# Float64 words of the weights made float32 by a scaling and three VectorE passes in place of a magnitude and four

## The chip, the cores and the metric

The kernel runs on one core of a Trainium2 chip. The core has a matrix engine (TensorE, written PE in the profile), a vector engine (VectorE, DVE), a scalar engine (ScalarE, ACT), GpSimd (POOL) and an engine that issues the transfers (SyncE, SP). Each takes its own instructions in the order in which the program gives them and waits at semaphores for the others. The metric is the device time of one execution in microseconds (us); lower is better.

## The reference

A windowed attention with global tokens, then two feed-forward layers over the 4 x (512 + 32) = 2176 token rows that the attention gives. Cut to what matters:

```
# attention: B=4, H=8, 512 local and 32 global tokens, head size 64, window 32
s_g   = scale * q_g @ concat(k_g, k_l)^T          ; out_g = softmax(s_g) @ concat(v_g, v_l)
s_l   = concat(scale * q_l @ k_g^T, where(|i - j| <= 32, scale * q_l @ k_l^T, -1e9))
out_l = softmax(s_l) @ concat(v_g, v_l)
x = concat(out_g, out_l) -> [2176, 512]
# first feed-forward layer, d_model 512, d_ff 2048
h = max(x @ w_in, 0);  x = (h * h) @ w_out
# second one
h = x @ w2_in
g = (a0 + a1*h + a2*h^2 + a3*h^3) / (1 + |b0|*|h| + |b1|*h^2 + 1e-6)
out = g @ w2_out
```

The four weight matrices arrive as float64. The chip's engines work in float32, so the kernel makes float32 words of the two 32-bit halves of each float64 word itself.

## The kernel before, in words

The order of the work is written out by hand: the program is one list, and each engine runs its own part of the list in that order.

**Attention, p = 0 to 15, and two more steps in which it drains.** Each `p` is a pair of heads. PE makes `scores` of two halves u = 0, 1; DVE finds their `maxima` (L308); ACT takes `exps` (L316); DVE adds 1e-9 to the sums (`sums`, L320) and takes their reciprocal (`norm`, L324); POOL multiplies the probabilities by it (L327, four instructions for a half); one step later PE transposes them (`transp`, L345 and L346), ACT and DVE copy the transposes out (L350, L352), and PE multiplies them by v (`pv`). On odd `p` the scores of the global queries (`g_scores`, L413 and L414) come between. They overwrite the banks that `maxima(p, 0, 0)` and `maxima(p, 0, 1)` read.

**Feed-forward.** The tokens are five tiles (512, 512, 384, 384, 384) for each of the two layers, and a tile goes through the 16 blocks of the hidden size (`s` counts tiles times blocks). At each `s` PE makes h for block s (`mm1`, L168 to L170) and the output product of block s - 3 (`mm2`, L181, LAG = 3). Every float32 product is made of three: x and the weights are split into a high and a low part. In the first layer ACT takes `max(h, 0)` out of PSUM (L210), DVE squares it (L211), ACT squares it again rounded to the high part `gh` (L212), and DVE subtracts to get the low part `gl` (L213), which `mm2` needs for its last eight products of a step.

**Weights.** There are 64 blocks of [128, 512] weights: 16 for `w_in` and 16 for `w_out` of each layer. A block is loaded by SP as 512 float64 words in each partition (`w_load`, three buffers `raw`). ACT takes the magnitude of the upper halves, read as float32 (`w_abs`, L90). DVE then makes four passes over `cv` (`w_float`): a floor (L101), a mask and a shift by 3 bits (L103), the sign and the top exponent bit from the upper halves (L105), three more mantissa bits from the lower halves (L108). After that the block is split: ACT writes the high part (L119; DVE in the attention, L117) and POOL subtracts for the low part (`w_rest`, L125). 13 of the 64 blocks are made in the attention, one for each `p` from 3 to 15, with the four passes placed apart as `step(0)` to `step(3)`. 19 more are made during the first token tile, in turns two and one for each `s`, ahead of `ew1(s)` on DVE:

```
            mm1(s)
            if j >= LAG:
                mm2(s - LAG)
            if t < NT - 1:
                floats(1)
            (ew1 if s < S1 else ew2)(s)
            if t < NT - 1:
                splits()
                if t == 0 and todo and todo[0][0] == 0:
                    magnitudes(2 - j % 2)
```

The other 32, of the second layer, are made in the tiles after that, and stored to memory until their turn.

Of the kernel before, what the change touches and what calls it, by code (L numbers as in the profile page):

```python
# [11 lines left out]
F32 = mybir.dt.float32  # L12
# [4 lines left out]
AF = mybir.ActivationFunctionType  # L17
ALU = mybir.AluOpType
# [24 lines left out]
EPS1 = 1.0 + 1e-6  # L43
SH = 60
N_IN0, N_OUT0 = 8, 5
TINY = float(np.array(0x38000000, np.uint32).view(np.float32))


def window(w):
# [4 lines left out]
def body(ctx, tc, qT, kW, v, w1i, w1o, w2i, w2o, coef, out):  # L54
    nc = tc.nc
    pe, act, dve, pool, sync = nc.tensor, nc.scalar, nc.vector, nc.gpsimd, nc.sync
# [21 lines left out]
    raws, cvs, have = {}, {}, {}  # L78
    stash = [[dram.tile([128, 512], F32, name=f"st{k}_{j}") for j in range(KF)] for k in range(2)]

    def w_load(ph, kind, j):
        raw = raw_p.tile([128, 512], I64, tag="raw", name="raw")
        src = ((w1i, w2i), (w1o, w2o))[kind][ph]
        sync.dma_start(raw, src[j])
        words = raw.bitcast(I32).rearrange("p (n t) -> p n t", t=2)
        raws[ph, kind, j] = words[:, :, 1], words[:, :, 0]

    def w_abs(ph, kind, j):
        f = t_p.tile([128, 512], F32, tag="t", name="cv")
        act.activation(f, raws[ph, kind, j][0].bitcast(F32), AF.Abs)  # L90
        cvs[ph, kind, j] = f

    def w_float(ph, kind, j, steps=(0, 1, 2, 3)):


        f = cvs[ph, kind, j]
        u = f.bitcast(I32)
        top, low = raws[ph, kind, j]
        for k in steps:
            if k == 0:  # L100
                dve.tensor_scalar(f, f, TINY, None, op0=ALU.max)  # L101
            elif k == 1:
                dve.tensor_scalar(u, u, 0x07FFFFFF, 3, op0=ALU.bitwise_and, op1=ALU.logical_shift_left)  # L103
            elif k == 2:
                dve.scalar_tensor_tensor(u, in0=top, scalar=-0x40000000, in1=u,  # L105
                                         op0=ALU.bitwise_and, op1=ALU.bitwise_or)
            else:
                dve.scalar_tensor_tensor(u, in0=low, scalar=29, in1=u,  # L108
                                         op0=ALU.logical_shift_right, op1=ALU.bitwise_or)
                del raws[ph, kind, j]  # L110
# [152 lines left out]
    def open_ff():  # L263
        qk_s.close()
        ff_p["ab"] = ctx.enter_context(tc.tile_pool(name="ab", bufs=2, side="right"))
        ff_p["g"] = ctx.enter_context(tc.tile_pool(name="g", bufs=LAG + 1, side="right"))
# [4 lines left out]
    def load_qk(p):  # L271
        b, hp = divmod(p, 4)
        qt[p] = qk_p.tile([128, SL + SG], F32, tag="q", name="q")
        kt[p] = qk_p.tile([128, KC], F32, tag="k", name="k")
        cuts = [(0, 0), (256, 576), (SL + SG, KC)] if p == 0 else [(0, 0), (SL + SG, KC)]
        for (q0, k0), (q1, k1) in zip(cuts, cuts[1:]):
            sync.dma_start(qt[p][:, q0:q1], qT[b, hp][:, q0:q1])
            sync.dma_start(kt[p][:, k0:k1], kW[b, hp][:, k0:k1])

    def load_v(g):  # L280
        b, hf = divmod(g, 2)
        vt[g] = v_p.tile([128, VC], F32, tag="v", name="v")
        sync.dma_start(vt[g], v[b, hf])
# [3 lines left out]
    def sm_tiles(p, u):  # L287
        sm[p, u] = (sm_p.tile([128, 2 * KW, 2], F32, tag="sm", name="sm"),
                    st_p.tile([128, 4], F32, tag="nm", name="nm"),
                    st_p.tile([128, 4], F32, tag="sum", name="sum"),  # L290
                    st_p.tile([128, 4], F32, tag="rs", name="rs"))

    def scores(p, u):
        for i in range(2):
            for j in range(2):
                for a in range(2):
                    r, w = slice(64 * j, 64 * j + 64), 4 * u + 2 * i + (a if i else 1 - a)
                    c = window(w) - 32 * i
                    pe.matmul(s_ps[2 * u + j][64 * a:64 * a + 64, KW * i:KW * i + KW],  # L299
                              qt[p][r, 64 * w:64 * w + 64], kt[p][r, c:c + KW],  # L300
                              start=True, stop=True, tile_position=(64 * j, 64 * a))

    def maxima(p, u, j):
        s, nm = sm[p, u][:2]
        for i in range(2):
            b, k = 2 * u + i, 2 * j + i
            o = s[:, KW * i:KW * i + KW, j]
            dve.tensor_tensor_reduce(out=o, in0=s_ps[2 * u + j][:, KW * i:KW * i + KW], in1=mask[:, b],  # L308
                                     scale=-0.125, scalar=3.0e38, op0=ALU.add, op1=ALU.min,
                                     accum_out=nm[:, k:k + 1])  # L310
# [8 lines left out]
    def sums(p, u):  # L319
        dve.tensor_scalar(sm[p, u][3], sm[p, u][2], 1e-9, None, op0=ALU.add)  # L320
# [130 lines left out]
    with tc.manual_schedule():  # L451
# [32 lines left out]
        early = [(0, 0, j) for j in range(N_IN0)] + [(0, 1, j) for j in range(N_OUT0)]  # L484
# [3 lines left out]
        for p in range(NP + 2):  # L488
            if p == NP:
                open_ff()  # L490
            if 1 <= p and p + 3 < NP:
                load_qk(p + 3)
            if p == 1:
                load_v(1)
            if p >= 4 and p % 2 == 0 and p // 2 < NP // 2:
                load_v(p // 2)
            if 1 <= p < 1 + len(early):
                w_load(*early[p - 1])
            n = p - 3
            cv = early[n] if 0 <= n < len(early) else None  # L500
            cur, pre = p < NP, 1 <= p <= NP
            odd = p % 2 == 1 and p + 2 < NP
            g = (p + 1) // 2

            def step(*k):
                if cv:
                    w_float(*cv, k)

            if cur:
                sm_tiles(p, 0)  # L510
                scores(p, 0)
                maxima(p, 0, 0)
                exps(p, 0, 0)
            else:
                mm1(p - NP)
            if 2 <= p:
                pv_local(p - 2, 0)
            if pre:
                sums(p - 1, 1)
            if cur:  # L520
                maxima(p, 0, 1)
            if pre:
                norm(p - 1, 1)
                p_tiles(p - 1, 0)
                p_tiles(p - 1, 1)
                if p > 1:
                    g_copies(p - 1, 0)
                    g_copies(p - 1, 1)
            step(0)
            if 2 <= p:  # L530
                pv_global(p - 2, 0)
            step(1)
            if p == 1:
                for k in range(4):
                    pe.matmul(tc_ps[0], warm[:, 0:128], warm, start=True, stop=True)
            if pre:
                transp(p - 1, 0)
                transp_evac(p - 1, 0)
            step(2)
            if cur:  # L540
                exps(p, 0, 1)
            if odd or p == 0:
                g_scores(g)
            if p == 1:
                g_transp(0)
                g_copies(0, 0)
                g_copies(0, 1)
            if 2 <= p:
                pv(p - 2, 1)
            if p % 2 == 0 and 0 < p < NP:  # L550
                g_transp(g)
            if cur:
                sm_tiles(p, 1)
                scores(p, 1)
                if odd or p == 0:
                    g_scale(g)
                    g_exps(g)
                maxima(p, 1, 0)
                sums(p, 0)
                step(3)  # L560
                norm(p, 0)
                exps(p, 1, 0)
                maxima(p, 1, 1)
            if odd or p == 0:
                g_norm(g)
            if cv:
                w_split(*cv, dve)
                w_rest(*cv)
            if 2 <= p:
                pv_local(p - 2, 1)  # L570
                pv_global(p - 2, 1)
            if pre:
                transp(p - 1, 1)
                transp_evac(p - 1, 1)
            if cur:
                exps(p, 1, 1)
            if pre:
                pv(p - 1, 0)
            if 0 <= n + 1 < len(early):
                w_abs(*early[n + 1])  # L580
            if 9 < p <= 9 + KD:
                x_low(0, p - 10)
            if 9 <= p < 9 + KD:
                x_high(0, p - 9)
            if p >= NP:
                ew1(p - NP)
# [26 lines left out]
        todo = []  # L613
# [22 lines left out]
        def magnitudes(k):  # L636
            for _ in range(k):
                if todo:
                    w_abs(*todo[0])
                    made.append(todo.pop(0))  # L640

        def splits():
# [25 lines left out]
        for s in range(2, 2 * S1):  # L668
            t, j = divmod(s, KF)
# [97 lines left out]
```

## Time and profile before

| | |
|---|---|
| time, median of 3 runs | 907.04 us (907.02 to 907.33) |
| the profiled execution's own time | 906.48 us |
| its span in the trace | 904.7 us |
| PE busy | 890.2 us (98%) |
| DVE busy | 662.7 us (73%) |
| ACT busy | 547.3 us (60%) |
| POOL busy | 258.8 us (29%) |

A busy share is a mean over the whole span. PE's share is high, but its instructions are pipelined, so one that waits for its operand can still count as busy; the other engines have stretches in which they are full and others in which they have little to do. The span is 1.8 us shorter than the time of the same execution, which holds what lies around it.

### The profile page before, as it was taken

What the parts mean: (1) busy time and instruction counts of PE and PEld (TensorE: products, weight loads), DVE (VectorE), ACT (ScalarE), POOL (GpSimd) and SP (SyncE); (2) the same over time, 40 slices, a digit from 0 to 9 for tenths busy, and PEclk for the clock granted to TensorE, in tenths of its full rate; (3) what the DMA queues carried; (4) which work ended last, traced back from release to release, by engine and by line L of the source; (5) the groups of instructions that cost most, each with busy time, mean ns of one, the idle gap of its engine ahead of it and who ended that gap; (6) DMA issues with size and microseconds to landing.
All of it is one profiled execution on the core that took longest, in us unless ns stands there. A gap on an engine that the chain in (4) does not pass through costs nothing.

```text
span 904.7 us, 14722 instructions
## 1 busy us (share of the span) xinstructions
PE 890.2 (98%) x5397; PEld 783.4 (87%) x5398; DVE 662.7 (73%) x1406; ACT 547.3 (60%) x1186; POOL 258.8 (29%) x324
## 2 busy tenths in 40 slices
PE   8999999997999999999999999999999999999998
PEld 4777778886888899999999978888888999999998
DVE  4788976999776568664332479877877888887886
ACT  5878874444433334342244568767766886886885
POOL 3667881334000000000036543221222222222221
PEclk9999999999999999999999999999999999999999
DMA  9767631333154327532014410001000100000001
GB/s 350 297 220 299 218 135 61 127 117 132 49 169 139 105 75 214 166 91 84 1 59 122 125 34 1 1 0 47 1 1 0 48 1 1 35 1 21 15 1 36
DMA packets 27576, 81.43 MB, mean 90 GB/s; under 512 B 3184, under 2 KB 4976, under 8 KB 26480
## 3 DMA queue, kind: packets, MB, share of 16 engines
q1 hardware_dynamic: 27504, 80.49, 26.3%
q8 instruction: 42, 0.69, 0.3%
q14 instruction: 30, 0.25, 0.1%
HBM read 67.64 MB, written 12.85 MB: 89 GB/s over the span
## 4 chain that ended last, share of the span: by engine, by line
PE 86%; DVE 10%; ACT 1%; issue 1%; DMA 1%; POOL 1%; SPq 0%; DVEq 0%; POOLq 0%; ACTq 0%
PE tc L181 19%; PE pv L181 19%; PE s L168 12%; PE s L169 12%; PE s L170 12%; PE pv L364 3%; PE tc L345 2%; DVE cv L105 2%; PE pv L370 2%; PE s L299 2%; DVE cv L101 2%; DVE cv L108 1%; DVE gl L213 1%; PE s L413 1%; DVE cv L103 1%
## 5 line engine op out<-in xcount | busy, mean ns | idle before, releaser
L168 PE MATMUL s<-xh,wi 128*128 128x384 f32 (+1 forms) x640 | 229.7, 359 | 0.0
L170 PE MATMUL s<-xh,wi 128*128 128x384 f32 (+1 forms) x640 | 228.4, 357 | 0.0
L169 PE MATMUL s<-xl,wi 128*128 128x384 f32 (+1 forms) x640 | 228.3, 357 | 0.0
L248 POOL TENSOR_TENSOR gl<-tt,gh 128x384 fp32r<-128x384 f32 (+1 forms) x79 | 89.9, 1137 | 268.1 <-ACT gh L247 207.0
L181 PE MATMUL tc<-gh,wo 128*128 128x384 f32 (+1 forms) x640 | 153.3, 361 | 0.8 <-ACT gh L247 0.8
L181 PE MATMUL pv<-gh,wo 128*128 128x384 f32 (+1 forms) x640 | 152.5, 360 | 0.0
L210 ACT ACTIVATE a<-s 128x384 f32<-128x384 f32 (+1 forms) x80 | 42.5, 532 | 153.1 <-PE s L170 153.0
L170 PEld LDWEIGHTS s<-xh,wi 128*128 128x128 f32 x640 | 120.1, 188 | 11.4
L169 PEld LDWEIGHTS s<-xl,wi 128*128 128x128 f32 x640 | 120.2, 188 | 10.8
L168 PEld LDWEIGHTS s<-xh,wi 128*128 128x128 f32 x640 | 120.1, 188 | 10.6
L181 PEld LDWEIGHTS tc<-gh,wo 128*128 128x128 f32 x640 | 116.4, 188 | 12.6 <-ACT gh L247 1.7
L181 PEld LDWEIGHTS pv<-gh,wo 128*128 128x128 f32 x640 | 115.9, 188 | 11.8
L211 DVE TENSOR_TENSOR b<-a 128x384 f32<-128x384 f32 (+1 forms) x80 | 50.3, 629 | 103.2 <-ACT a L210 103.2
L125 POOL TENSOR_TENSOR wi<-raw,wi 128x512 fp32r<-128x512 f32 x16 | 21.4, 1337 | 267.2 <-ACT wi L119 247.2
L181 PE MATMUL tc<-gl,wo 128*128 128x384 f32 (+1 forms) x320 | 89.9, 362 | 4.6 <-DVE gl L213 4.6
L181 PE MATMUL pv<-gl,wo 128*128 128x384 f32 (+1 forms) x320 | 89.8, 361 | 0.0
L225 DVE SCALAR_TENSOR_TENSOR a<-a,nf,b 128x384 f32<-128x384 f32 (+1 forms) x80 | 53.4, 667 | 32.3 <-ACT b L223 32.2
L327 POOL TENSOR_SCALAR sm<-sm,rs 128x160 f32<-128x160 f32 x128 | 63.6, 521 | 38.1 <-DVE rs L324 13.1
L222 ACT ACTIVATE a<-s 128x384 f32<-128x384 f32 (+1 forms) x80 | 42.0, 525 | 52.8 <-PE s L170 52.8
L181 PEld LDWEIGHTS tc<-gl,wo 128*128 128x128 f32 x320 | 58.7, 188 | 11.3 <-DVE gl L213 5.5
L238 DVE SCALAR_TENSOR_TENSOR a<-a,b 128x384 f32<-128x384 f32 (+1 forms) x80 | 49.0, 612 | 22.0 <-ACT b L233 22.0
L181 PEld LDWEIGHTS pv<-gl,wo 128*128 128x128 f32 x320 | 58.9, 188 | 5.9
(115 smaller groups left out, 1449.7 us busy)
## 6 DMA issues: line engine op xcount, KB each, us to landing
v<-in_v_dram SPq DMA_DIRECT2D x8, 1408.0 KB, 7.9
k<-in_kW_dram SPq DMA_DIRECT2D x15, 592.0 KB, 5.6
raw<-in_w1i_dram SPq DMA_DIRECT2D x16, 512.0 KB, 5.1
raw<-in_w1o_dram SPq DMA_DIRECT2D x16, 512.0 KB, 3.5
raw<-in_w2i_dram SPq DMA_DIRECT2D x16, 512.0 KB, 3.9
st<-cv SPq DMA_DIRECT2D x32, 256.0 KB, 4.2
raw<-in_w2o_dram SPq DMA_DIRECT2D x16, 512.0 KB, 4.0
raw<-st SPq DMA_DIRECT2D x32, 256.0 KB, 2.6
```

The lines of the kernel that those rows point to most:

```text
L168: pe.matmul(ph, wh, hi[:, kk, :n], start=(kk == 0), stop=False)
L169: pe.matmul(ph, wh, lo[:, kk, :n], start=False, stop=False)
L170: pe.matmul(ph, wl, hi[:, kk, :n], start=False, stop=(kk == KD - 1))
L181: pe.matmul(acc_bank[d][:, :n], w[:, half, 128 * d:128 * d + 128], src[:, :n], start=start, stop=stop)
L210: act.activation(a, ph, AF.Relu)
L211: dve.tensor_tensor(b, a, a, op=ALU.mult)
L222: act.activation(a, ph, AF.Square)
L225: dve.scalar_tensor_tensor(a, in0=a, scalar=nf[:, 5:6], in1=b, op0=ALU.mult, op1=ALU.add)
L238: dve.scalar_tensor_tensor(a, in0=a, scalar=EPS1, in1=b, op0=ALU.add, op1=ALU.mult)
L248: eng.tensor_tensor(gl, t, gh.bitcast(F32), op=ALU.subtract)
L327: pool.tensor_scalar(e, e, rs[:, k:k + 1], 1.0, op0=ALU.mult, op1=ALU.mult)
L364: pe.matmul(bank[64 * j:64 * j + 64, o0:o1], v[:, VW * w + 64 * jj:VW * w + 64 * jj + 64], p1[:, j, o0 + (32 if o0 >= 128 else 0):o1 + (32 ...
```

## The change

What it does: ACT no longer takes the magnitude of the upper half but multiplies it by 2^-112, with its sign. That puts the exponent where a shift by 3 bits needs it. The floor pass goes, and the mask in front of the shift goes; the shift alone is the first pass now. The second pass takes the sign bit alone from the upper half, and the third is the last one of before. In the attention, `step(0)` to `step(2)` issue the three passes, and `step(3)`, which stood between `sums(p, 0)` and `norm(p, 0)`, is gone.

```
-    def w_abs(ph, kind, j):
+    def w_scale(ph, kind, j):
         f = t_p.tile([128, 512], F32, tag="t", name="cv")
-        act.activation(f, raws[ph, kind, j][0].bitcast(F32), AF.Abs)
+        act.activation(f, raws[ph, kind, j][0].bitcast(F32), AF.Copy, scale=2.0 ** -112)
         cvs[ph, kind, j] = f

-    def w_float(ph, kind, j, steps=(0, 1, 2, 3)):
+    def w_float(ph, kind, j, steps=(0, 1, 2)):
...
             if k == 0:
-                dve.tensor_scalar(f, f, TINY, None, op0=ALU.max)
+                dve.tensor_scalar(u, u, 3, None, op0=ALU.logical_shift_left)
             elif k == 1:
-                dve.tensor_scalar(u, u, 0x07FFFFFF, 3, op0=ALU.bitwise_and, op1=ALU.logical_shift_left)
-            elif k == 2:
-                dve.scalar_tensor_tensor(u, in0=top, scalar=-0x40000000, in1=u,
+                dve.scalar_tensor_tensor(u, in0=top, scalar=-0x80000000, in1=u,
                                          op0=ALU.bitwise_and, op1=ALU.bitwise_or)
             else:
                 dve.scalar_tensor_tensor(u, in0=low, scalar=29, in1=u,
                                          op0=ALU.logical_shift_right, op1=ALU.bitwise_or)
...
                 sums(p, 0)
-                step(3)
                 norm(p, 0)
```

The lines of the changed file stand one to three lower from here on (L105 is L103, L108 is L106, L308 is L306, L320 is L318, L324 is L322, L211 is L209). On DVE, in one step of the attention (p = 12), this stood between the reciprocal of the step before and that of this one. cv and raw are the block in conversion, p and x are the attention's copies, sm, nm, sum and rs those of the softmax:

```order
L101 TENSOR_SCALAR cv<-cv 128x512
L396 COPY x<-pv_94 128x32
L103 TENSOR_SCALAR cv<-cv 128x512
L352 COPY p_1695<-tc_93 128x128
L105 SCALAR_TENSOR_TENSOR cv<-raw,cv 128x512
...
L320 TENSOR_SCALAR rs<-sum 128x4
L108 SCALAR_TENSOR_TENSOR cv<-raw,cv 128x512
L324 RECIPROCAL rs<-rs 128x4
```

The same place on DVE in the changed kernel (left out in both are the maxima of the first bank of half 1):

```order
L101 TENSOR_SCALAR cv<-cv 128x512
L394 COPY x<-pv_94 128x32
L103 SCALAR_TENSOR_TENSOR cv<-raw,cv 128x512
L350 COPY p_1686<-tc_93 128x128
L106 SCALAR_TENSOR_TENSOR cv<-raw,cv 128x512
...
L318 TENSOR_SCALAR rs<-sum 128x4
L322 RECIPROCAL rs<-rs 128x4
```

A two-source pass now stands ahead of the copy of the transposes, where the mask and shift stood, and nothing of the conversion is left between `sums` and the reciprocal.

On DVE in the first token tile, one step with two conversions before, between the elementwise work of one block and that of the next (b, gl: the square and its low part):

```order
L211 TENSOR_TENSOR b_2409<-a_2408 128x512
L213 TENSOR_TENSOR gl_2411<-b_2409,gh_2410 128x512
L101 TENSOR_SCALAR cv_2418<-cv_2418 128x512
L103 TENSOR_SCALAR cv_2418<-cv_2418 128x512
L105 SCALAR_TENSOR_TENSOR cv_2418<-raw_2356,cv_2418 128x512
L108 SCALAR_TENSOR_TENSOR cv_2418<-raw_2356,cv_2418 128x512
L101 TENSOR_SCALAR cv_2420<-cv_2420 128x512
L103 TENSOR_SCALAR cv_2420<-cv_2420 128x512
L105 SCALAR_TENSOR_TENSOR cv_2420<-raw_2362,cv_2420 128x512
L108 SCALAR_TENSOR_TENSOR cv_2420<-raw_2362,cv_2420 128x512
L211 TENSOR_TENSOR b_2459<-a_2458 128x512
L213 TENSOR_TENSOR gl_2461<-b_2459,gh_2460 128x512
```

The same step on DVE in the changed kernel:

```order
L209 TENSOR_TENSOR b_2391<-a_2390 128x512
L211 TENSOR_TENSOR gl_2393<-b_2391,gh_2392 128x512
L101 TENSOR_SCALAR cv_2400<-cv_2400 128x512
L103 SCALAR_TENSOR_TENSOR cv_2400<-raw_2340,cv_2400 128x512
L106 SCALAR_TENSOR_TENSOR cv_2400<-raw_2340,cv_2400 128x512
L101 TENSOR_SCALAR cv_2402<-cv_2402 128x512
L103 SCALAR_TENSOR_TENSOR cv_2402<-raw_2345,cv_2402 128x512
L106 SCALAR_TENSOR_TENSOR cv_2402<-raw_2345,cv_2402 128x512
L209 TENSOR_TENSOR b_2439<-a_2438 128x512
L211 TENSOR_TENSOR gl_2441<-b_2439,gh_2440 128x512
```

Nothing changes places there; of each conversion one pass is gone. The other engines keep their instructions in number and order.

## Rows read from the trace of the kernel before

**Rows 1.** Stretches of the span: busy us and (instructions) of each engine, then clock.

```profile
30.00:130.00 100.00, 97.99 (x1203) 72.03 (x1198) 88.72 (x396) 82.53 (x303) 77.49 (x143) 1.00 0.64 235
145.00:232.00 87.00, 82.39 (x350) 66.09 (x349) 82.82 (x110) 40.75 (x73) 31.00 (x19) 0.98 0.33 115
232.00:420.00 188.00, 188.00 (x955) 170.93 (x954) 125.09 (x224) 69.41 (x128) 0.00 (x0) 1.00 0.43 131
```

**Rows 2.** Waits of PE, 140 to 905 us: waited for, us, times, longest.

```profile
PE tc L181 <- DVE gl L213: 4.6, 2, 4.2
```

**Rows 3.** Timeline of PE, 216 to 234 us: start, us, instruction, idle before.

```profile
225.41 1.22 PE L181 MATMUL tc<-gl,wo 128*128 128x512 f32 x2 [4.22 <-DVE gl L213]
...
230.55 1.10 PE L181 MATMUL tc<-gh,wo 128*128 128x512 f32 x4
...
233.35 0.40 PE L168 MATMUL s<-xh,wi 128*128 128x512 f32 x1
```

**Rows 4.** Stretches of 1 us behind that wait: PE, PEld, DVE, ACT, POOL, clock.

```profile
226.00:227.00 1.00, 1.00 (x4) 0.81 (x3) 1.00 (x1) 0.97 (x3) 0.48 (x1) 0.50 0.58 234
```

**Rows 5.** Single lines, 144 to 232 us: min/median/max ns, first and last start.

```profile
L101 DVE TENSOR_SCALAR cv<-cv x19: 418/1516/1528, 145.8 to 220.6; 128x512 f32<-128x512 f32 x19
L90 ACT ACTIVATE cv<-raw x19: 647/656/672, 145.1 to 217.0; 128x512 f32<-128x512 f32 x19
L119 ACT ACTIVATE wo<-cv x11: 630/632/635, 151.6 to 224.0; 128x512 fp32r<-128x512 f32 x11
```

**Rows 6.** Timeline of DVE, 183 to 197 us.

```profile
191.45 1.53 DVE L101 TENSOR_SCALAR cv<-cv 128x512 f32<-128x512 f32 x1
193.01 0.43 DVE L103 TENSOR_SCALAR cv<-cv 128x512 int32<-128x512 int32 x1
193.47 0.69 DVE L105 SCALAR_TENSOR_TENSOR cv<-raw,cv 128x512 int32<-128x512 int32 x1
...
195.73 1.75 DVE L105 SCALAR_TENSOR_TENSOR cv<-raw,cv 128x512 int32<-128x512 int32 x1
```

**Rows 7.** Timeline of POOL, the same stretch.

```profile
190.85 1.84 POOL L125 TENSOR_TENSOR wi<-cv,wi 128x512 fp32r<-128x512 f32 x1 [2.94 <-ACT wi L119]
195.64 1.30 POOL L125 TENSOR_TENSOR wo<-cv,wo 128x512 fp32r<-128x512 f32 x1 [2.95 <-ACT wo L119]
```

**Rows 8.** The chain that ended last, in order of time, first and second token tile.

```profile
161.01 1.46 DVE cv L101
...
173.88 1.45 DVE cv L101
...
249.99 0.94 PE tc L181 x4
...
255.55 0.94 PE tc L181 x4
```

**Rows 9.** The same chain in the attention.

```profile
76.78 0.78 DVE rs L320
...
98.46 0.59 DVE cv L108
```

**Rows 10.** Timeline of DVE in the attention, 72 to 84 us.

```profile
73.47 0.84 DVE L108 SCALAR_TENSOR_TENSOR cv<-raw,cv 128x512 int32<-128x512 int32 x1
74.23 0.17 DVE L324 RECIPROCAL rs<-rs 128x4 f32<-128x4 f32 x1
...
76.20 0.33 DVE L308 CUSTOM_DVE_ANT_0 sm<-s,mask 128x160 f32<-128x160 f32 x1 [0.65 <-PE s L299]
...
76.69 0.86 DVE L320 TENSOR_SCALAR rs<-sum 128x4 f32<-128x4 f32 x1
```

**Rows 11.** Timeline of POOL, the same stretch.

```profile
74.57 1.73 POOL L327 TENSOR_SCALAR sm<-sm,rs 128x160 f32<-128x160 f32 x4 [0.80 <-ACT x L389]
76.25 1.28 POOL L125 TENSOR_TENSOR wi<-cv,wi 128x512 fp32r<-128x512 f32 x1
```

**Rows 12.** Longest wait of PE's loads in the attention, 30 to 130 us.

```profile
PEld tc L345 <- POOL sm L327: 5.2, 20, 0.6
```

More of the change, by code (lines that the diff above doesn't have):

```diff
@@ L45 @@
 N_IN0, N_OUT0 = 8, 5
-TINY = float(np.array(0x38000000, np.uint32).view(np.float32))
 def window(w):
@@ L579, in body @@
             if 0 <= n + 1 < len(early):
-                w_abs(*early[n + 1])
+                w_scale(*early[n + 1])
             if 9 < p <= 9 + KD:
@@ L638, in magnitudes @@
                 if todo:
-                    w_abs(*todo[0])
+                    w_scale(*todo[0])
                     made.append(todo.pop(0))
```

## The prediction, made before the changed kernel ran

> **What bounds the kernel now.** I read the stretches first. From 232 to 420 us PE is busy for all of 188.00 us although DVE still makes 32 blocks there; where PE is full, a shorter DVE gives nothing [rows 1]. Two stretches are left. In the first token tile (145 to 232 us) DVE is busy for 82.82 of 87 us and PE for 82.39 [rows 1]. In the attention (30 to 130 us) no engine is idle for long: DVE 88.72, ACT 82.53, POOL 77.49 of 100 us, and the 97.99 of PE are padded by products that wait while they count as busy [rows 1].
>
> Then the waits of PE. From 140 us to the end, `gl` (L213 on DVE) holds it up twice, 4.6 us together [rows 2]. The longer one, 4.22 us, ends at 225.41 us [rows 3], and behind it the granted clock is 0.50, which is 1.2 of 2.4 GHz [rows 4]. From 225.41 to 233.35 PE runs 28 products in 7.94 us; the last 12 of them, at full clock, take 230.55 to 233.35, 2.80 us or 0.233 each [rows 3]. At that rate 28 would take 6.53, so the slow clock costs 1.41 us. The hole costs 4.6 + 1.4 = 6.0 us.
>
> Why there is a hole: on DVE the same pass of the two-and-one rhythm stands at 161.01 and at 173.88 us, 12.87 us apart, with three conversions and two blocks of elementwise work in between. PE needs 5.56 us for a step (249.99 to 255.55), 11.12 for two [rows 8]. DVE falls 1.75 us further behind in each pair, about 10 us in the 75 us between the first and the last start of L101 [rows 5]; the lag of three steps hides it until almost the end.
>
> In the attention the chain runs over PE for most of its length. Where it leaves PE it names DVE and POOL: the small pass L320 takes 0.78 us (three times, about 16 us apart, 76.78 the last of them), the fourth conversion pass L108 takes 0.59, ahead of the reciprocal that POOL waits for (twice, at 98.46 and 114.53), and then PE waits for POOL's L327 [rows 9]. PE's weight loads wait 5.2 us for L327 in the 100 us, in 20 waits [rows 12].
>
> **The change part by part.** *The pass that goes.* It looks as if L101 were dear: 1516 ns in the median of the tile [rows 5]. But the 1.53 us at 191.45 lie on POOL's L125, which started at 190.85 and ended at 192.69 [rows 6, 7]; where POOL rests it is near its minimum, 418 ns [rows 5]. L105, with 0.69 us otherwise, takes 1.75 us at 195.73 when L125 has just begun at 195.64 [rows 6, 7]. So the wait goes with POOL's subtraction and not with the pass. The shift that now comes first will stand in it. I credit one unstalled pass for each conversion: 193.01 to 193.47, 0.46 us [rows 6]. If the whole 1.53 us went, two steps on DVE would take about 12.87 - 2 x 1.5 - 0.5 = 9.4 us; with 0.46 they take 12.87 - 3 x 0.46 = 11.5.
>
> The Trainium skill (SBUF — State Buffer, Who interferes with whom) says that VectorE and GpSimd share a pair of ports as an exclusive lock, for one-source passes in the two-port mode and for passes with two SBUF inputs: whoever comes second is blocked until the other is done. By it the wait moves to the pass that comes next, and two steps take the 11.5 us; these rows agree with it.
>
> *The shift alone.* The trace has no shift without a mask. From below: the one-source passes L103 (0.43) and L101 (0.42). From above: a two-source pass, 0.69 [rows 5, 6]. It has the shape, the place and the type of L103, so I take 0.43.
>
> *The tile.* After the change DVE needs 11.5 us for what PE does in 11.12: it still falls behind, 0.4 us a pair, some 2.2 us over the tile in place of 10. The `gl` that comes 4.22 us too late has 19 conversions ahead of it [rows 5]. It comes 19 x 0.46 = 8.7 us earlier. Where the second of two conversions has POOL's subtraction break in at another pass, perhaps 0.38 is left of the 0.46: then 7.2 us. Both are over 4.6, so the hole goes with its slow clock: -6.0 us. Behind it nothing else is near: the low part of the next block would be early by the same 7 to 8 us.
>
> *ACT.* L90 goes from a magnitude to a copy with a scale. The nearest rows are itself (656 ns) and L119, a copy of the same length (632) [rows 5]. That is between nothing and 0.02 us for each block, off the path, for ACT is busy for 40.75 of 87 us [rows 1]. I take nothing; if L90 were 0.1 us slower, the 1.1 us for which the pass behind it stands at POOL's lock would cover it [rows 6].
>
> *The attention.* Each of 13 steps loses a pass, and `step(3)` with its 0.61 to 0.77 us between `sums` and the reciprocal is empty. Where the chain stands on it (98.46 and 114.53) the gain is 0.59 each, 1.2 us [rows 9]. On the odd steps before those: L108 at 73.47 holds up the reciprocal at 74.23, POOL's L327 at 74.57 waits for that, L125 stands behind L327 on POOL (76.25 to 77.53), and L320 on DVE at 76.69 is blocked by L125 until then, 0.86 us for four columns [rows 10, 11]. With L108 out of that place everything on POOL comes 0.6 earlier (POOL was idle 0.80 us before, so it can [rows 11]), L125 ends at about 76.9, and of L320's 0.78 about 0.6 goes: three times, 1.8 us. The other 5.2 us in which PE's weight loads wait for L327 [rows 12] hang on the same earlier start in half of the cases (the half whose norm stood behind L108), and ACT and DVE have little room left to follow; I take 1.0. The sum is 1.2 + 1.8 + 1.0 = 4.0 us. Its bounds: nothing, if the next engine fills in at once; and 13 x 0.61 = 7.9 us, if each step is a loop through that place.
>
> What it costs there: a two-source pass (0.61 from start to start of the next) stands where the mask and shift (0.45) stood, ahead of the copy L352 and the maxima of the global scores. 0.16 us later, on a DVE that waits 0.65 us for PE's scores a little later anyway [rows 10]. Uncovered, 13 x 0.16 = 2.1 us.
>
> *DMA.* The same loads in the same order. A buffer `raw` is free a pass earlier; no wait of PE hangs on a load [rows 2].
>
> *Sum.* Against the profiled execution: 906.48 - 6.0 - 4.0 = 896.5 us. The median is 0.56 higher, so 897.0.
>
> **Rivals.**
> *Only the hole closes.* The attention is a pipeline of four nearly full engines; ACT at 82.53 and POOL at 77.49 of 100 us keep their work. What DVE gives back may turn into idle time of DVE. For it: DVE waits for PE's scores in each step already. Against: POOL has idle time just before L327, and only the reciprocal ends it. Time 907.04 - 6.0 - 0 to 1.5 = 899.5 to 901.0.
> *Every step gains the whole pass.* 907.04 - 6.0 - 7.9 = 893.1. For it: L327 ends 20 waits of PE's weight loads [rows 12]. Against: the chain names L108 twice, not 13 times.
> *The shift is slow.* At 0.69 us each conversion gains 0.20, 19 of them 3.8 us, less than 4.6: a hole of about 0.8 to 1 us with a part of its slow clock stays, and the attention gives about 2. 907.04 - 4.5 - 2 = 900.5; without the gain in the attention 902.5.
> *Nothing.* POOL's lock, not DVE's passes, sets the rhythm of the tile: then DVE's gain is swallowed by a longer stall. Against it: after a stalled L101 two unstalled passes and the elementwise work follow, all of it on the chain, so a pass less is time less. 907.
> *Slower.* POOL's L125, shifted by 0.6 us, may now start just ahead of a pass that PE waits for: the maxima cannot be stalled by it as far as the trace shows, but the reciprocal and L320 can, for up to L125's 1.28 us in a step [rows 11]. For 13 steps that is up to 16 us; from 10 / 13 = 0.8 us a step on it outweighs what I forecast, and at 1.0 us the time is 907.04 - 6.0 + 13 x 1.0 - 4.0 = 910. Against it: today's place is such a collision (L320, 0.78 on the chain), and the shift leads away from it, into the 0.65 us in which DVE waits for PE [rows 10].
>
> **How the numbers follow.** The forecast, hole closed and 1.5 to 6 us from the attention (895 to 899.5): 0.52. Only the hole: 0.17. Every step: 0.14. Slow shift or a hole half closed: 0.09. Nothing: 0.03. Slower: 0.05. The range takes in the first three and most of the fourth, 892.0 to 902.5, and leaves out about 1 in 7. A measurement tells some 0.2% (1.8 us) of this kernel from no change: faster 0.92, the same 0.03, slower 0.05.
>
> **What would show it.** PE's waits for `gl` near 212 and 221 us gone, and the clock at 1.00 through the tile. The first pass of a conversion at about 1.5 us where L125 runs and at 0.43 elsewhere; the rhythm on DVE 11.5 us or, if DVE keeps up, PE's 11.12. In the attention L320 at 0.2 us on odd steps, L327 starting right behind the sums, and the first product of the feed-forward some 4 us earlier than now. From 232 us on nothing but a shift. The forecast is wrong if the wait at L213 is still there (a slow shift, or another stall), or if the attention ends when it did.

## The result, and the profile after

The changed kernel takes 899.36 us in the median (898.96 to 899.53, 4 runs), the kernel before 907.03 beside it (906.43 to 907.33, 4 runs). The ratio is 0.9916, 95% interval 0.9898 to 0.9933. That is 7.7 us faster; 10 were forecast (897.0), with a range of 892.0 to 902.5. The hole went as forecast. In the attention 0.6 us was gained where the forecast had 4.0. Another 0.6 of the 7.7 us lies in the start, ahead of the steps that make blocks, and differs from trace to trace.

The page of the profiled execution of the changed kernel, its span and busy times:

```profile
span 897.0 us, 14659 instructions
PE 888.1 (99%) x5398; PEld 781.9 (87%) x5398; DVE 635.3 (71%) x1342; ACT 547.8 (61%) x1186; POOL 262.5 (29%) x324
```

The stretches that answer to [rows 1]: length, then PE, PEld, DVE, ACT, POOL, the clock, and DMA.

```profile
30.00:130.00 100.00, 98.05 (x1211) 72.00 (x1208) 82.52 (x386) 83.20 (x306) 80.83 (x147) 1.00 0.65 237
145.00:232.00 87.00, 87.00 (x377) 70.51 (x377) 75.70 (x94) 42.49 (x75) 32.29 (x19) 1.00 0.35 115
```

From 145 to 232 us PE is now full at a clock of 1.00, so the slow clock of [rows 4] has gone. In the attention DVE is busy for 6 us less and POOL for 3 us more, and PE is hardly fuller.

PE's waits from 130 us on, where [rows 2] stood, have one row left. It is the wait for the high part in the second layer, which the kernel before has too:

```profile
PE tc L179 <- ACT gh L245: 0.8, 2, 0.6
```

PE's timeline gives three marks by which every trace here can be cut: the first product of the global scores of p = 3, the first of the feed-forward, and the first of the second token tile. For the changed kernel:

```profile
28.23 1.30 PE L411 MATMUL s<-k,q 64*32 64x512 f32 x5
...
129.93 0.50 PE L166 MATMUL s<-xh,wi 128*128 128x512 f32 x1
...
225.68 0.40 PE L166 MATMUL s<-xh,wi 128*128 128x512 f32 x1
```

In the kernel before they stand at 28.81, 131.14 and 233.35 us. So the attention took 102.33 and takes 101.70 us, the first tile took 102.21 and takes 95.75. The 0.58 us by which the first mark differs are there before DVE's first pass over a block (28.75 us; ACT's first is at 27.4 and was at 28.0); over all traces of this study that mark lies between 27.39 and 29.41 us.

The single lines on DVE and ACT from 130 to 232 us, which answer to [rows 5], minimum, median and maximum in ns:

```profile
L101 DVE TENSOR_SCALAR cv<-cv x19: 419/1517/1528, 144.6 to 210.5; 128x512 int32<-128x512 int32 x19
L106 DVE SCALAR_TENSOR_TENSOR cv<-raw,cv x19: 691/693/1670, 145.8 to 211.7; 128x512 int32<-128x512 int32 x19
L89 ACT ACTIVATE cv<-raw x19: 650/656/672, 143.9 to 207.4; 128x512 f32<-128x512 f32 x19
```

And DVE's timeline in the tile, for [rows 6]:

```profile
191.86 1.52 DVE L101 TENSOR_SCALAR cv<-cv 128x512 int32<-128x512 int32 x1
193.41 0.69 DVE L103 SCALAR_TENSOR_TENSOR cv<-raw,cv 128x512 int32<-128x512 int32 x1
194.14 0.69 DVE L106 SCALAR_TENSOR_TENSOR cv<-raw,cv 128x512 int32<-128x512 int32 x1
...
203.27 1.52 DVE L101 TENSOR_SCALAR cv<-cv 128x512 int32<-128x512 int32 x1
```

And POOL's, of the subtraction that meets the first of them:

```profile
191.26 1.84 POOL L123 TENSOR_TENSOR wi<-cv,wi 128x512 fp32r<-128x512 f32 x1 [1.29 <-ACT wi L117]
```

The shift alone takes 419 ns at the least, and 1.52 us where POOL's subtraction runs: the stall passed from the floor to the shift. The rhythm of two steps is 203.27 - 191.86 = 11.41 us (11.5 forecast, 12.87 before).

Where the attention's gain went is seen in the chain that ended last, from 34 to 41 us, the start of an even step (p = 4):

```profile
35.72 0.33 DVE sm L306
...
36.29 1.20 DVE rs L318
...
38.63 1.67 POOL sm L325 x2
40.29 0.04 issue
40.34 0.77 PE tc L343 x2
```

The small pass L318 (L320 before) is on the chain again, now with 1.20 us, and after it POOL's norm, for which PE waits. The same four pieces come at 52.25, 68.23 and 84.20 us. POOL's timeline there:

```profile
35.50 0.72 POOL L432 TENSOR_SCALAR gs<-gs,gm 128x544 f32<-128x544 f32 x1
36.20 1.27 POOL L123 TENSOR_TENSOR wi<-cv,wi 128x512 fp32r<-128x512 f32 x1
```

and DVE's:

```profile
36.21 1.28 DVE L318 TENSOR_SCALAR rs<-sum 128x4 f32<-128x4 f32 x1
```

L318 comes 0.01 us behind the start of POOL's subtraction and stands until it is over. Before, the block fell on the odd steps, with 0.78 us on the chain, as the second part of the subtraction was left [rows 9, 10, 11]. On the even steps L320 came ahead of the subtraction and stood for 0.50 us, until POOL's norm of the global scores (L434, 36.55 to 37.27 us) was over; the chain did not go over it:

```profile
36.78 0.50 DVE L320 TENSOR_SCALAR rs<-sum 128x4 f32<-128x4 f32 x1
37.23 1.27 POOL L125 TENSOR_TENSOR wi<-cv,wi 128x512 fp32r<-128x512 f32 x1
```

Behind p = 10 the chain of the changed kernel runs over POOL itself, twice (98 to 104 and 114 to 121 us); the first time:

```profile
98.84 1.50 POOL sm L325 x2
100.34 0.68 POOL gs L432
101.02 0.64 POOL wo L123
101.99 0.26 issue
102.25 2.24 POOL sm L325 x3
104.53 0.77 PE tc L343 x2
```

### The profile page after: what moved, and what is told of

It reads as the page before. It is cut to its first block, busy times and chain, and to the rows that moved or that the text cites. A ratio compares the mean times of both kernels' runs of the same rounds, so it can differ in the third digit from the quotient of the medians.

```text
span 897.0 us, 14659 instructions
## 1 busy us (share of the span) xinstructions
PE 888.1 (99%) x5398; PEld 781.9 (87%) x5398; DVE 635.3 (71%) x1342; ACT 547.8 (61%) x1186; POOL 262.5 (29%) x324
## 4 chain that ended last, share of the span: by engine, by line
PE 93%; POOL 2%; DVE 2%; issue 1%; ACT 1%; DMA 1%; SPq 0%; POOLq 0%; ACTq 0%
PE tc L179 21%; PE pv L179 21%; PE s L166 14%; PE s L168 14%; PE s L167 14%; PE pv L362 2%; POOL sm L325 2%; PE tc L343 2%; PE pv L368 2%; PE s L297 2%; PE s L411 1%; DMA k<-in_kW_dram 1%; DVE sm L306 1%; DVE rs L318 1%; DVE tt L237 0%
## 5 line engine op out<-in xcount | busy, mean ns | idle before, releaser
L209 DVE TENSOR_TENSOR b<-a 128x384 f32<-128x384 f32 (+1 forms) x80 | 50.4, 630 | 117.9 <-ACT a L208 117.9
L179 PEld LDWEIGHTS pv<-gh,wo 128*128 128x128 f32 x640 | 115.9, 188 | 11.8
L325 POOL TENSOR_SCALAR sm<-sm,rs 128x160 f32<-128x160 f32 x128 | 66.4, 542 | 34.5 <-ACT sm L314 19.2
L314 ACT ACTIVATE sm<-sm,nm 128x160 f32<-128x160 f32 x128 | 55.6, 441 | 14.0 <-DVE nm L306 13.8
```

Of the source, the lines that this page charges most:

```text
L179: pe.matmul(acc_bank[d][:, :n], w[:, half, 128 * d:128 * d + 128], src[:, :n], start=start, stop=stop)
L209: dve.tensor_tensor(b, a, a, op=ALU.mult)
L314: act.activation(e, e, AF.Exp, scale=-1.0, bias=nm[:, k:k + 1], accum_out=tot[:, k:k + 1])
L325: pool.tensor_scalar(e, e, rs[:, k:k + 1], 1.0, op0=ALU.mult, op1=ALU.mult)
```

## The experiments

All medians are set against runs of the kernel before on the same chip. The attention and the tile are cut by the three marks of PE.

| kernel | median us | ratio to before, 95% | attention us | first tile us |
|---|---|---|---|---|
| before | 907.03 | | 102.33 | 102.21 |
| changed | 899.36 | 0.9916 (0.9898 to 0.9933) | 101.70 | 95.75 |
| e1 attention old | 900.67 | 0.9925 (0.9912 to 0.9939) | 102.44 | 95.79 |
| e2 tile old | 906.05 | 0.9988 (0.9980 to 0.9997) | 101.55 | 102.94 |
| e3 no small pass | 893.10 | 0.9845 (0.9831 to 0.9858) | 96.39 | 95.77 |
| e4 subtraction on DVE | 895.69 | 0.9871 (0.9858 to 0.9885) | 97.95 | 95.77 |
| e5 third pass in its old place | 900.21 | 0.9925 (0.9913 to 0.9937) | 101.32 | 95.77 |
| e6 before, tile's subtraction on DVE | 900.02 | 0.9924 (0.9910 to 0.9938) | 102.46 | 95.76 |
| e7 half the blocks old | 899.22 | 0.9915 (0.9901 to 0.9928) | 101.63 | 95.93 |
| e9 before, no small pass | 902.13 | 0.9951 (0.9938 to 0.9963) | 97.93 | 102.41 |
| e8 e3 and e4 together | 892.50 | 0.9842 (0.9829 to 0.9856) | 95.93 | 95.76 |

Kernels with the same attention lie within 0.15 us of each other there (102.33, 102.44, 102.46; 101.70, 101.63, 101.55), and those without a hole within 0.2 us in the tile. So the traces tell tenths which the times do not. The tiles with a hole spread further, 102.21 to 102.94, at the same wait of 4.6 us: behind it the granted clock stays low for a shorter or longer time (from 228 to 229 us it is 0.84 before and 0.50 in e2).

**e1, the attention's blocks in the old way.** For them `w_scale` and `w_float` are those of before, and `step(3)` is back:

```
+    def w_old(ph, kind, j):
+        return ph == 0 and j < (N_OUT0 if kind else N_IN0)
...
+        if w_old(ph, kind, j):
+            act.activation(f, raws[ph, kind, j][0].bitcast(F32), AF.Abs)
...
                 sums(p, 0)
+                step(3)
                 norm(p, 0)
```

> The 13 blocks of the attention are made in the old way (magnitude, four passes, in the old places), all others in the new way. If the two gains are separate, this one has the tile's alone: first product of the feed-forward where it is before (131.1 us in the trace), no wait for gl, 907.03 - 6.4 = 900.6 us. If the attention's shorter work is needed to close the hole (an earlier start of the tile, other buffers), a wait for gl of up to 4 us is left: 903 to 905.

900.67 us: the gains are separate, and the tile's alone is 907.41 - 900.67 = 6.7 us by the medians, 6.42 by the marks.

**e2, the other way round.** The attention's blocks are made with three passes, all later ones with four.

> The 13 blocks of the attention are made in the new way, all others in the old way. If the gains are separate: the attention ends 0.6 to 1.2 us earlier than before, the wait for gl stays at about 4.6 us with the clock at 1.2 GHz behind it, 906.0 us. If the tile's hole hangs on when the attention ends, the wait changes by as much as the attention gains, and the time does not move: 907.

906.05 us. PE's wait for `gl` is what it was, 4.6 us in two pieces:

```profile
PE tc L200 <- DVE gl L232: 4.6, 2, 4.2
```

The attention alone is worth 0.8 us by the marks, 1.1 (0.3 to 1.8) by the ratio. The two ratios of e1 and e2 multiply to 0.9913; the change has 0.9916.

**e3, no small pass for the lock to catch.**

```
     def sums(p, u):
-        dve.tensor_scalar(sm[p, u][3], sm[p, u][2], 1e-9, None, op0=ALU.add)
+        pass
...
-        dve.reciprocal(rs, rs)
+        dve.reciprocal(rs, sm[p, u][2])
```

> The changed kernel without the small pass that adds 1e-9 to the softmax sums (each sum is at least 1): the reciprocal reads the sums. That pass, L318, is blocked for 1.2 us by POOL's subtraction on five even steps. Theory lock: the attention's missing 3 us went into that block; without a pass for the lock to catch, the first product of the feed-forward starts 2 to 4 us earlier than 129.9, and the time is 895.5 to 897.5 us. Rival full: the attention is held by its four full engines and the block only fills time in which DVE would wait anyway: 899.0 to 899.5. Third: the reciprocal is caught in its place: 899.4, and L322 shows 1.2 us.

893.10 us, more than the theory of the lock had. The attention is 5.3 us shorter than in the changed kernel. In the trace POOL's subtraction still starts at the same kind of place:

```profile
36.94 1.30 POOL L123 TENSOR_TENSOR wi<-cv,wi 128x512 fp32r<-128x512 f32 x1
```

DVE's rows there:

```profile
37.75 0.17 DVE L322 RECIPROCAL rs<-sum 128x4 f32<-128x4 f32 x1
37.84 0.68 DVE L101 TENSOR_SCALAR cv<-cv 128x512 int32<-128x512 int32 x1
```

The reciprocal, of the same four columns, runs in the middle of the subtraction and takes its usual 0.17 us; only the shift behind it waits. So the third theory fell: the reciprocal is not caught, and neither were the maxima. Two things are taken away here, the block and the pass itself, 0.08 us on the chain of the kernel before where it is free (98.38 us); 26 times that, two in each of 13 steps, would be 2.1 us, an estimate from above.

**e4, POOL's subtraction moved to DVE in the attention.** The pass stays, what blocks it goes:

```
             if cv:
                 w_split(*cv, dve)
-                w_rest(*cv)
+                w_rest(*cv, dve)
```

> The changed kernel with the low part of the attention's 13 blocks subtracted by DVE (a two-source pass of 0.69 us) and not by POOL (1.28 us). Theory lock: L318 and the first pass are nowhere blocked for a whole subtraction, POOL's norm starts earlier, DVE has 0.61 more and up to 1.2 less in a step: first product 2 to 4 us earlier, 895.5 to 897.5 us. Rival full with DVE as the fullest engine: 13 x 0.61 more on DVE, up to 8 us later: 900 to 907. Rival full with another engine: 899.0 to 899.8.

895.69 us, within what the lock theory gave. From 28 us on L318 takes 332 ns at the most in place of 1283, and the attention is 3.75 us shorter although DVE has 13 passes of 0.69 us more: its busy time from 30 to 125 us is 83.94 us, as much as before the change (83.72). So it is not DVE's amount of work that held the attention. POOL has less to do here as well (70.00 us busy in the same stretch, 76.28 in the changed kernel); e8 shows what that is worth once the small pass is gone.

**e5, the third pass back between the sums and the reciprocal.**

```
-            step(2)
             if cur:
                 exps(p, 0, 1)
...
                 sums(p, 0)
+                step(2)
                 norm(p, 0)
```

> The changed kernel with the attention's third pass back between the sums and the reciprocal, where the fourth pass stood: three passes in the steps 0, 1 and 3. Theory place: what the attention gained or lost comes from emptying that place, which lets POOL's norm and subtraction start 0.6 us earlier and puts the subtraction under L318 on even steps. With the place filled again L318 is blocked as in the kernel before (0.8 us on odd steps) and the length from the global scores of p = 3 to the first product of the feed-forward is 102.0 to 102.4 us as before, time 899.5 to 900.5. Rival count: a pass less on DVE is what counts, wherever it stood: 101.5 to 101.8, time 899.2 to 899.6. If the lock costs more in the new place than it saved: below 101, time under 899.

The attention takes 101.32 us, below both windows of the two theories but not below 101. With the place filled L318 is blocked by up to 949 ns, and the chain has it with 0.85 us on the odd steps, as before. By the marks the pass less is worth 1.0 us there; emptying the place, on which the forecast built its gain, then lost 0.4. The times (900.21 and 899.36, in two sets of runs) cannot tell these apart.

**e6, the kernel before, with the subtraction of the first tile's blocks on DVE.** Four passes are left:

```
             act.activation(w[:, 0], f, AF.Copy)
-            w_rest(ph, kind, j)
+            w_rest(ph, kind, j, pool if ph else dve)
```

> The kernel before, four passes, with the low part of the first tile's 19 blocks (and of no others) subtracted by DVE and not by POOL. A two-source pass on DVE is 0.72 us from start to start; if the stalls of 1.07 us in the tile belong to POOL's subtraction and the lock, they all go, L101 is 0.42 and L105 0.69 everywhere, and the rhythm of two steps is 12.87 - 3 x 0.35 = 11.8 us: the hole closes without the change, 907.0 - 6 = 900.5 to 901.5. Rival: the first pass after the elementwise work is slow by itself (it waits for ACT's write or its buffer): then DVE has 3 x 0.72 more in two steps, 15.0 us, and the hole grows by some 12 us: 915 to 920.

900.02 us, 0.5 below what was expected: the hole is gone without the change. DVE has a pass more and no stall; the first pass of the conversion, 140 to 232 us:

```profile
L101 DVE TENSOR_SCALAR cv<-cv x19: 417/420/427, 145.7 to 212.1; 128x512 f32<-128x512 f32 x19
```

Its 1.52 us belonged to POOL's subtraction, then. The rhythm of two steps:

```profile
187.00 0.42 DVE L101 TENSOR_SCALAR cv<-cv 128x512 f32<-128x512 f32 x1
...
198.42 0.42 DVE L101 TENSOR_SCALAR cv<-cv 128x512 f32<-128x512 f32 x1
```

11.42 us; the expectation had 11.8, with 0.72 for a pass that costs 0.61 from start to start where it stands.

**e7, half the dose.** 9 of the tile's 19 blocks in the old way.

```
+    def w_old(ph, kind, j):
+        return ph == 0 and not (ph == 0 and j < (N_OUT0 if kind else N_IN0)) and j % 2 == 0
...
+        if w_old(ph, kind, j):
+            act.activation(f, raws[ph, kind, j][0].bitcast(F32), AF.Abs)
...
```

> The changed kernel with 9 of the 19 blocks of the first tile made in the old way (magnitude, four passes), those of even number. If only the sum of DVE's time in the tile counts, gl comes 10 x 0.46 = 4.6 us earlier than before, as much as the two waits were: the hole is just closed or a few tenths long, first product of the first tile to that of the second 95.7 to 96.5 us, time 899.3 to 900.5. If half the passes give half the gain, 99 us and 902.5.

899.22 us and 95.93 in the tile; no product waits for `gl`, and PE's weight loads wait for it once, 0.3 us. Ten passes less do what nineteen do: the sum of DVE's time up to the late `gl` counts, and the change has almost double of what the hole needed.

**e9, the kernel before without the small pass.** The edit of e3.

> The kernel before, without the small pass that adds 1e-9 to the sums. From the global scores of p = 3 to the first product of the feed-forward it was 102.3 us before, 101.7 in the changed kernel, 96.4 in the changed kernel without that pass. Theory lock: the pass less is worth some 4 us in the attention as soon as the lock has no small pass to catch; then this kernel takes 100 to 100.5 us there, and 904.5 to 905.5. Rival: the catch costs the kernel before as much as the changed one, and the pass less is worth 0.6 us either way: 97 us here and 901.5.

902.13 us, the attention 97.93: far from the theory's 100 to 100.5 and 0.9 above the rival's 97. The small pass and its block cost the kernel before 4.4 us, the changed one 5.3. With it out of the way the change is worth 97.93 - 96.39 = 1.5 us in the attention, not the theory's 4 and not the rival's 0.6.

**e8, e3 and e4 together**, the shortest median of all.

> The changed kernel without the small pass that adds 1e-9 to the sums, and with the low part of the attention's 13 blocks subtracted by DVE. The first alone brought the attention (global scores of p = 3 to the first product of the feed-forward) from 101.7 to 96.4 us, the second alone to 98.0. In the first POOL is busy for 82.65 of the 95 us from 30 to 125, ACT for 82.95. Theory POOL: POOL's queue is what holds the attention once the small pass is gone; with 13 x 1.28 us less on it the attention takes 93.5 to 95.5 us, 890.3 to 892.2. Rival ACT or PE's products: no room is left, 96.0 to 96.8 and 892.8 to 893.5. Rival DVE: 13 x 0.61 us more there show, above 97 and 894.

892.50 us (892.20 to 893.71), the attention 95.93, a little under the window of "no room is left" and above that of POOL. POOL is relieved, from 30 to 122 us without it and with it:

```profile
30.00:122.00 92.00, 91.75 (x1181) 69.43 (x1179) 72.50 (x349) 80.53 (x297) 79.65 (x140) 1.00 0.70 257
```

```profile
30.00:122.00 92.00, 91.35 (x1181) 69.45 (x1179) 79.23 (x369) 80.53 (x297) 70.65 (x131) 1.00 0.70 252
```

POOL's 9 us less gave 0.5 us by the marks, so with the small pass gone POOL's amount of work is worth no more than that. From 40 to 75 us the chain is all PE; the period of two steps is 14.95 us (42.36 to 57.31), where it was about 16. That PE's own products are what is left there is read from the chain; it was not tried by itself. From 94 us on the chain leaves PE again, above all for POOL's L325 (2.71 us at 99.77). The times of e3 and e8 overlap; which is the faster stays open.

## Why the prediction was right or wrong

**The hole: right.** The pass that goes was credited with 0.46 us and not with the 1.5 it seemed to take. The stall stayed (1517 ns in the median), the rhythm came to 11.41 us, the wait and the slow clock went. The rule cited from the Trainium skill (SBUF — State Buffer, Who interferes with whom) is borne out by e6: without POOL's subtraction in the tile no pass is slow. The tile gave 6.46 us where the sum had 6.0. The 0.4 more lies at the waits: from one first product of `mm1` to that of the next, the step with the shorter wait took 6.22 us (207.38 to 213.60) and not 5.56, 0.66 for a wait that the trace shows with 0.40. So a product that waits counts as busy for a part of it. The four blocks of `mm2` with the longer wait took 17.00 us and take 11.20, 5.80 where the sum had 4.22 and 1.41.

**The shift alone, and ACT: right.** 419 ns (0.43 taken). L89 kept its 656 ns.

**The dose: right, with more room than needed.** 8.7 us were worked out against 4.6, and e7 shows that about half was enough.

**The attention: wrong in size, 0.63 us for 4.0.** The step that failed is this one: "With L108 out of that place everything on POOL comes 0.6 earlier [...], L125 ends at about 76.9, and of L320's 0.78 about 0.6 goes: three times". On the odd steps it did go. But the subtraction that runs into an even step stands on POOL behind the norm of the global scores, and there the same earlier start brought it, 0.45 us behind the start of the small pass before (37.23 and 36.78), to the very start of it (36.20 and 36.21): 1.20 us on the chain, in four of the steps to p = 10. The rows of the prediction show the block of an odd step alone. The slower rival had this mechanism (the subtraction started just ahead of L320), and I set it aside because "the shift leads away from it"; that holds for odd steps alone.

The marks of four kernels part the 3.4 us that are missing. The small pass with its block costs 4.4 us before (e9) and 5.3 after (e3): it was to fall by 1.8 and rose by 0.9, which is 2.7 of them. The two other terms, 1.2 and 1.0, came to 1.5 with nothing to catch (e9 against e3), which is the other 0.7. For those PE is close behind: two steps take 15.33 us in e9 (44.40 to 59.73), 15.06 in e3 (44.39 to 59.45), 14.95 in e8, where the chain is all PE. The term of 1.2 did not arrive whole either. From the first `pv` product behind the global scores of p = 11 to that of p = 13, where L108 had stood on the chain at 98.46, the kernel before took 16.06 us (95.15 to 111.21) and the changed one 16.28 (94.37 to 110.65): POOL's own work is on the chain there. From p = 13 to the first product of the feed-forward, past the other L108 (114.53), 19.93 became 19.28.

**The rivals.** "Only the hole closes", at 0 to 1.5 us from the attention, is what happened (899.36 against 899.5 to 901.0), though not for its reason: the four engines were not full, for e3 took 5.3 us out of the attention by one pass of four columns. "Every step gains the whole pass", "the shift is slow" and "nothing" fell with the marks, the 419 ns and e6.

**Luck.** The time lies inside the range and even in the forecast's own bracket (895 to 899.5), which wanted 1.5 us or more from the attention. It got there with 0.63: in the traces the tile gave 0.46 more than its sum, and 0.58 came from the start, which no pass of the change touches.

## What to carry to other kernels

When a pass goes from an engine that waits at a lock shared with another, count what the pass takes unblocked; the stall passes to whatever comes next. Moving work earlier on one side of such a lock must be checked in every kind of step, since it decides which pass of the other side is caught, and a pass of four columns can cost as much as a block of weights. Before shortening large passes on a chain, look for small ones that stand on it blocked: here one pass was worth 5.3 us and the change 0.6 at the same place.

## What was not expected of the hardware

A one-source pass over [128, 4] (L318), 0.16 us by itself, is held for up to 1.28 us by a POOL subtraction, while a reciprocal of the same four columns is never over 0.18 us in the 27 of e3 from 28 us on, seven of which lie inside a subtraction. The two look alike in the program and differ by 1 us on the chain; the prediction's "the reciprocal and L320 can" holds for L320 alone.
